# A fixed instruction order from a table, and state transfers with 32 entries outermost

## The chip, the cores and the metric

The kernel runs on one core of one Trainium2 chip. The metric is the device time in microseconds (us): the median of three runs, each one execution of the whole program. A profiled execution gives the trace; its span is the time from the first instruction to the last.

## What is computed

Eight batches go through two stages. In the first, 512 rows of x and 32 rows of state attend to each other, separately for each of 8 heads of width 64. The two results are put one below the other (544 rows). In the second, a mixture of four attention experts runs over those rows, causal, with two experts chosen for each row.

```
x [8, 8, 512, 64], state [8, 8, 32, 64]        # batch, head, row, width
scores  = x @ state^T / 8        ; xread = softmax(scores) @ state       # 512 rows
scores2 = state @ x^T / 8        ; sread = softmax(scores2) @ x          # 32 rows
X = concat([xread, sread], rows), heads side by side                     # [8, 544, 512]
logits = X @ w_gate              ; the two largest of four experts, softmax over the two
for each expert e: q, k, v = X @ wq[e], X @ wk[e], X @ wv[e]
    y = softmax(causal(q @ k^T / 8)) @ v @ wo[e]
    out += (weight of e for the row) * y                                 # [8, 544, 512]
```

## The kernel before, in words

Every value that is multiplied on TensorE (PE) is split into two fp16 parts, high and low, and a product is made of three matmuls (`PROD`). The work of a batch is written as steps. `front(b)` loads x (`xn`) and the state (`sn`), splits x into `xh`, turns it with DMA transposes (`xT`), makes the first softmax (`eb`, `at`), the gate (`lg`, `gt1`, `gt2`, `wgt`; `gate`) and the masked queries, keys and values (`qm`, `kt`, `v`). `side(b)` makes the softmax of the 32 state rows: the exponentials `e2`, the weights `a2`, and their transpose `a2t`. `probs(b, i)` does block i of 128 rows: scores, exponentials `p32`, the split parts `ph`, and a DMA transpose into `pt`. `reads(b, i)` multiplies `pt` with `v`, scales on VectorE (DVE) into `z32`, adds two halves of `z32` on GpSimd (POOL) or DVE, splits the sum into `zh`, transposes it by DMA into `z`, multiplies with `wo_n`, copies the result out of PSUM on ScalarE (ACT) into a tile `o`, and stores it in two stores of 64 rows. `tail(g)` does the state rows of a pair of batches (`tq`, `ptl`, `tpt`, `tzr`, `tz`); every second call stores the 32 state rows of four batches from one tile `o`.

All DMAs are issued by the sync engine (SP), whose queue is in order. `b` in a name of the trace is cut: `p` stands for `p32`, `a` for `a2`, `e` for `e2`, `z` for `z32` and for `z`, `m` for `m2` and `m6`.

Nothing in the code says directly in which order the steps are issued. `Steps.step` records each step with its engine, its estimated duration, and, for some, a choice of engines (`either`). When all are recorded, `Steps.run` orders them: `plan` is a list scheduler with estimated times, `replay` scores a plan with added delays, 12 rounds of forward and backward planning and 100 random changes follow, and the best plan is emitted. The plan decides three things: the order on each engine, the engine where there is a choice, and the buffer slot of each tile. Where it sees PE idle for more than 0.5 us it also puts in filler matmuls on zeros (line 477). Since all steps are emitted in `run`, nearly every row of the trace carries line 479, and the steps are told apart by the names of their tiles.

The two transfers that the change touches are the load of one half of the heads' states and the store of the state rows:

```
st.dma(sns[b // 2][:, b % 2, c], state[b].rearrange("(j c) n d -> c j n d", c=2)[c], 0.6, after=after)
st.dma(out[(g_ - 1) * NB:(g_ + 1) * NB, S:S + NS, :], o, 0.73)
```

In the first, the outermost dimension of the DRAM side is j, four heads; in the second it is the batch, four of them.

Of the kernel before, what the change touches and what calls it, by code (L numbers as in the profile page):

```python
# [15 lines left out]
ALU = mybir.AluOpType  # L16
# [10 lines left out]
LN = math.log(2.0 ** 15)  # L27

# [57 lines left out]
class Steps:  # L86
# [7 lines left out]
    FILL = 0.0535  # L94

    KEEP = 3.0
    START, LANDED, TICK = 0.65, 0.93, 10.24 / 3
    LANDS = (1.4, 2.0, 2.6)
    SIGNAL = {"PE": 0.2, "ACT": 0.16, "DVE": 0.14, "POOL": 0.1, "SP": 0.0}

    def __init__(self, nc, sb, psum):
        self.nc, self.pools, self.tags, self.all = nc, {False: sb, True: psum}, {}, []
        self.base, self.scale, self.clock, self.kind, self.lines = 0.0, 1.0, 0.0, "", {}
        self.behind = None
        self.lean = {"DVE": 0.0, "ACT": 0.0, "POOL": 0.0}
        self.patience = dict.fromkeys(("PE", "DVE", "ACT", "POOL", "SP"), 0.0)
# [17 lines left out]
    def step(self, eng, dur, calls, reads, writes, land=0.0, after=None, ways=None, issue=0.0, modes=(None, None)):  # L124
        s = dict(modes=modes, eng=eng, dur=dur, calls=calls, ways=[(*w, self.takes_port(w[0], w[2])) for w in ways or [(eng, dur, calls, 0.0)]], want=self.base + self.scale * self.clock, n=len(self.all),
# [42 lines left out]
    def dma(self, out, in_, transfer, transpose=False, after=None):  # L168
# [3 lines left out]
        return self.step("SP", max(1.18, transfer + 0.35) if transpose else issue, [(f, dict(out=out, in_=in_))], [v for v in (in_,) if isinstance(v, View)],  # L172
                         [v for v in (out,) if isinstance(v, View)], land=transfer, after=after, issue=issue)
# [32 lines left out]
    def plan(self, want, ways=None, back=False, until=None):  # L206

        steps = self.all  # L210
        after, before = self.links
        then = before if back else after
        waits = [len(x) for x in (after if back else before)]
        ready = [0.0] * len(steps)
        free = dict.fromkeys(("PE", "DVE", "ACT", "POOL", "SP"), 0.0)
        if not back:
            free.update(SP=0.62, POOL=1.14, DVE=1.5, ACT=1.5, PE=0.94)
        dma_free = 0.0
        mode = None
        port = 0.0  # L220
        counts = []
        open_ = {e: [] for e in free}
        pool = {tag: [(0.0, i) for i in range(len(slots))] for tag, slots in self.tags.items()}
        line = {k: (n[0] - 1 if back else 0) for k, n in self.lines.items()}
        fills = {}
        slot, left, last = {}, {i: b.left for i, b in self.bufs.items()}, {}
        used = self.used

        def opens(n):
            for e in ([steps[n]["ways"][ways[n]][0]] if ways else [w[0] for w in steps[n]["ways"]]):  # L230
                open_[e].append(n)

        for n in range(len(steps)):
            if not waits[n]:
                opens(n)

        def start(n):
            t = ready[n]
            need = {}
            for i in used[n]:  # L240
                if i not in slot:
                    b = self.bufs[i]
                    if line[b.turn[0]] != b.turn[1]:
                        return None
                    need[b.tag] = need.get(b.tag, 0) + 1
            for tag, k in need.items():
                p = pool[tag]
                if len(p) < k:
                    return None
                t = max(t, p[k - 1][0])  # L250
            return t

        def held(way):
            return (free["POOL"] if way[0] == "DVE" else port) if way[4] else 0.0

        order = []
        while len(order) < len(steps):
            best = None
            for e, cand in open_.items():
                now, mine = free[e], []  # L260
                for n in cand:
                    t = start(n)
                    if t is None:
                        continue
                    w = steps[n]["ways"]
                    if ways:
                        t = max(t, now, held(w[ways[n]]))
                    else:
                        cost = {x[0]: max(t, free[x[0]], held(x)) for x in w}
                        if len(w) > 1 and e != min(w, key=lambda x: cost[x[0]] + x[1] + x[3])[0]:  # L270
                            continue
                        t = cost[e]
                    mine.append((t, want[n] + (self.KEEP if e == "PE" and steps[n]["modes"][-1 if back else 0] != mode else 0.0), n))
                if mine:
                    t = min(mine)[0] + self.patience[e]
                    t, _, n = min((m for m in mine if m[0] <= t), key=lambda m: m[1:])
                    if best is None or t < best[0]:
                        best = t, n, e
            if best is None and back:

                short = {self.bufs[i].tag for c in open_.values() for n in c for i in used[n] if i not in slot}
                assert short
                for tag in short:
                    pool[tag].append((max(o[3] for o in order), 0))
                continue
            if best is None:
                return 1e9, order, slot, fills
            t, n, e = best
            s = steps[n]
            for i, w in enumerate(s["ways"]):  # L290
                if n in open_[w[0]]:
                    open_[w[0]].remove(n)
                if w[0] == e:
                    way, dur = i, w[1]
            clear = None
            for i in used[n]:
                if i not in slot:
                    b = self.bufs[i]
                    if b.tag == "bank" and clear is None:
                        clear = pool[b.tag][0][0]  # L300
                    slot[i] = pool[b.tag].pop(0)[1]
                    line[b.turn[0]] += -1 if back else 1
            if e == "PE":
                first, last_ = s["modes"][::-1] if back else s["modes"]
                dur += self.SWITCH * (first != mode)
                mode = last_
            end = t + dur
            if e == "PE" and not back and clear is not None:
                at = max(clear, free["PE"])
                if t - at > 0.5:  # L310
                    fills[n] = 0
                    while True:
# [3 lines left out]
                        if at > t - 0.15:  # L316
                            break
# [166 lines left out]
def state_read_then_moe_attention(ctx: ExitStack, tc: tile.TileContext, x, state, w_gate, wq, wk, wv, wo, out):  # L484
# [13 lines left out]
    P = 128  # L498
# [697 lines left out]
```

## Time and profile before

| | |
|---|---|
| three runs | 331.86, 332.98, 334.36 us (median 332.98) |
| profiled execution, span | 329.7 us; the page gives no other time of this execution, so what lies around the span is told by the median, 3.3 us above it |
| PE busy | 301.7 us, 92% |
| DVE busy | 265.6 us, 81% |
| ACT, POOL busy | 212.0 us (64%), 197.5 us (60%) |
| DMA queue 1 | 77.9% of the time of 16 engines |
| mean granted TensorE clock | 0.989 |

PE's busy time overstates its work, since the matmuls are pipelined and one that is held back in the pipeline still counts. A share of a whole span is a mean over stretches with different limits, so it is read by stretches.

### The profile page before, as it was taken

Reading aid. Unit: us, or ns where it says so; the run is one execution under the profiler, and the core shown is the slowest. Engines: PE = TensorE matmul, PEld = TensorE weight load, DVE = VectorE, ACT = ScalarE, POOL = GpSimd, SP = SyncE. Lnnn points to the kernel's source line nnn. Section 1 sums busy time; section 2 is a strip of 40 time slices with the busy share of each in tenths; the row PEclk is TensorE's granted clock in tenths of the full one; section 3 lists DMA queues with packets and bytes.
Section 4 is the critical chain, followed back from the end, with each engine's and each line's share of the span. In section 5 each row is a group of like instructions: output and inputs, shape, how many; then the busy total and the mean of one; then the engine's idle time right before and its main releaser. Section 6 shows DMA issues by size and latency. Waiting matters only on the chain.

```text
span 329.7 us, 10132 instructions
## 1 busy us (share of the span) xinstructions
PE 301.7 (92%) x3906; PEld 201.3 (61%) x3906; DVE 265.6 (81%) x850; ACT 212.0 (64%) x483; POOL 197.5 (60%) x267
## 2 busy tenths in 40 slices
PE   7999599899996999978999997999999999999991
PEld 7786275586454655755456754857546846686750
DVE  3789899999998997995789994998988875894430
ACT  4676697585747859556668874866866756365330
POOL 7044286397864877955868960969965844645400
PEclk9999999999999999999799999999999999999997
DMA  8949909983898999999749898397789867408754
GB/s 192 198 108 164 219 10 166 219 115 66 125 194 196 156 164 154 214 162 233 129 96 148 153 230 116 71 145 156 146 149 188 115 127 119 88 20 171 143 127 95
DMA packets 140712, 47.72 MB, mean 145 GB/s; under 512 B 119672, under 2 KB 136056, under 8 KB 140664
## 3 DMA queue, kind: packets, MB, share of 16 engines
q1 hardware_dynamic: 140664, 47.08, 77.9%
q8 instruction: 30, 0.49, 0.6%
q14 instruction: 18, 0.15, 0.2%
HBM read 11.02 MB, written 8.91 MB: 60 GB/s over the span
## 4 chain that ended last, share of the span: by engine, by line
DVE 37%; PE 27%; ACT 13%; DMA 12%; issue 5%; POOL 4%; SPq 1%; ACTq 0%; DVEq 0%; POOLq 0%
PE bank L479 25%; DVE mx L479 4%; DMA pt<-ph 4%; DVE xh L479 3%; DVE qf L479 3%; DVE gs L479 3%; DVE m L479 3%; DVE a L479 2%; DVE sbm L479 2%; DVE eb L479 2%; DMA p<-in_moe_wo_dram 2%; DVE z L479 2%; ACT xh L479 2%; ACT p L479 2%; DMA xn<-in_x_dram 2%
## 5 line engine op out<-in xcount | busy, mean ns | idle before, releaser
L479 PE MATMUL bank<-kt,qm 64*128 64x128 f16 (+7 forms) x384 | 50.8, 303 | 0.8 <-ACT p L479 0.3
L479 PE MATMUL bank<-v,pt 128*128 128x193 f16 x480 | 44.9, 247 | 2.5 <-DMA pt<-ph 1.3
L479 PE MATMUL bank<-wo_n,z 128*128 128x512 f16 x192 | 45.8, 379 | 0.9 <-DMA z<-zh 0.9
L479 PEld LDWEIGHTS <-pt 128*128 128x128 f16 x480 | 40.2, 98 | 8.0 <-issue 3.2
L479 PE MATMUL bank<-at,gs 128*128 128x512 f16 x192 | 44.6, 379 | 0.0
L479 ACT ACTIVATE p<-bank,mx 128x256 f32<-128x256 f32 (+3 forms) x64 | 31.8, 525 | 15.0 <-DVE mx L479 10.5
L479 POOL TENSOR_TENSOR ph<-p,ph 128x256 f16<-128x256 f32 (+3 forms) x24 | 32.2, 1344 | 9.8 <-ACT ph L479 9.3
L479 PEld LDWEIGHTS <-qm 64*128 64x128 f16 (+1 forms) x384 | 22.3, 96 | 17.4 <-issue 5.1
L479 ACT ACTIVATE o<-bank 128x512 f32<-128x512 f32 x34 | 20.0, 593 | 18.0 <-PE bank L479 17.9
L479 POOL TENSOR_TENSOR qm<-qf,qm 128x512 f16<-128x512 f32 x23 | 26.9, 1187 | 6.2 <-ACT qm L479 4.4
L479 PE MATMUL bank<-gs,at 128*128 128x4 f16 (+1 forms) x384 | 29.9, 218 | 0.7 <-DVE mx L479 0.5
L479 DVE TENSOR_REDUCE mx<-bank 128x1 f32<-128x128 f32 (+3 forms) x64 | 28.2, 475 | 2.5 <-PE bank L479 2.3
L479 PEld LDWEIGHTS <-z 128*128 128x128 f16 x192 | 17.7, 98 | 20.0 <-DMA z<-zh 1.6
L479 PEld LDWEIGHTS <-gs 128*128 128x128 f16 x192 | 17.6, 97 | 19.8 <-issue 1.1
L479 PEld LDWEIGHTS <-at 128*128 128x128 f16 x384 | 23.7, 97 | 5.9 <-issue 1.9
L479 POOL TENSOR_TENSOR zh<-z,zh 128x256 f16<-128x256 f32 x29 | 20.3, 700 | 6.1 <-ACT zh L479 5.6
L479 POOL TENSOR_TENSOR z<-z 128x128 f32<-128x128 f32 x32 | 17.1, 538 | 9.1 <-DVE z L479 4.8
L479 ACT ACTIVATE ph<-p 128x256 f16<-128x256 f32 (+3 forms) x26 | 18.7, 722 | 5.9 <-DMA pt<-ph 5.5
L479 DVE SCALAR_TENSOR_TENSOR xh<-xn,xh 128x512 f16<-128x512 f32 x22 | 18.8, 873 | 4.2 <-ACT xh L479 4.0
L479 ACT ACTIVATE xh<-xn 128x512 f16<-128x512 f32 x32 | 19.1, 626 | 4.5 <-DMA xn<-in_x_dram 4.4
L479 DVE TENSOR_TENSOR qf<-bank,mt 64x512 f32<-64x512 f32 (+1 forms) x32 | 21.1, 684 | 1.1 <-ACT mt L479 0.6
L479 POOL TENSOR_TENSOR eb<-eb,sbm 128x512 f32<-128x512 f32 x14 | 15.0, 1080 | 6.9 <-DVE sbm L479 5.4
(175 smaller groups left out, 677.6 us busy)
## 6 DMA issues: line engine op xcount, KB each, us to landing
xn<-in_x_dram SPq DMA_DIRECT2D x16, 512.0 KB
out_dram<-o SPq DMA_DIRECT2D x64, 128.0 KB
sn<-in_state_dram SPq DMA_DIRECT2D x16, 32.0 KB
p<-in_moe_wo_dram SPq DMA_DIRECT2D x2, 256.0 KB
pt<-ph SPq DMA_TRANSPOSE x32
out_dram<-o SPq DMA_DIRECT2D x2, 256.0 KB
z<-zh SPq DMA_TRANSPOSE x29
xT<-xh SPq DMA_TRANSPOSE x28
```

The lines of the kernel that those rows point to most:

```text
L479: f(**{k: v.ap() if isinstance(v, View) else v for k, v in kw.items()})
```

## The change

The planner (`plan`, `replay`, the search in `run`) is gone. In its place stand two tables. `ORDER` lists all 2036 steps in the order in which they are to be issued, each as number.way.fillers: the number of the step as recorded, which of its engines is taken, and how many filler matmuls go ahead of it. `SLOTS` gives the buffer slot of each tile. Whoever made the tables ran a longer search, with a model of the DMA queue. The code that records the steps is the same but for the two transfers, which have a dimension of 32 state rows outermost, and what follows from that: the partitions of a loaded state are in the order (row, head), and PE's transpose of it is read in another order (`byhead`); the state rows of a pair of batches in `zr` are interleaved (`both`); and one store of four batches is now two stores of two.

```diff
+ORDER = """
+3.0 0.0 1.0 2.0 4.0 68.0 70.0 67.0 11.0 7.0 16.0 12.0 10.0 8.0 17.0 13.0.6 9.0 18.0 14.0 15.1 69.0 21.0 20.0 19.1 22.0 26.0 74.0.23 73.0 27.0 72.0
...
+SLOTS = {
+    "xn": "0101011001101010",
...
-    def run(self, rounds, climbs, tries=8):
...
+    def run(self):
+
+        order = [entry.split(".") for entry in ORDER.split()]
+        left = {i: iter(slots) for i, slots in SLOTS.items()}
+        assert len(order) == len(self.all)
+        for entry in order:
+            s = self.all[int(entry[0])]
+            calls = s["ways"][int(entry[1])][2]
+            for b in s["bufs"].values():
+                if b.slot is None:
+                    b.slot = self.tags[b.tag][int(next(left[b.tag])) if b.tag in left else 0]
+            if len(entry) > 2:
+                to = next(kw["out"].buf.slot for _, kw in calls)
+                for _ in range(int(entry[2])):
                     self.nc.tensor.matmul(out=to[:, :128], lhsT=self.zeros, rhs=self.zeros, start=True, stop=True, skip_group_check=True)
-            for f, kw in s["ways"][way][2]:
+            for f, kw in calls:
                 f(**{k: v.ap() if isinstance(v, View) else v for k, v in kw.items()})
...
-            select(both[r, c * NS:(c + 1) * NS], ALU.not_equal, 1.0, 0, [[-1, NS]], 1)
+            select(both[r, c:NB * NS:NB], ALU.not_equal, 1.0, 0, [[-1, NS]], 1)
...
-            st.dma(sns[b // 2][:, b % 2, c], state[b].rearrange("(j c) n d -> c j n d", c=2)[c], 0.6, after=after)
+            st.dma(sns[b // 2][:, b % 2, c], state[b].rearrange("(j c) n d -> c n j d", c=2)[c], 0.2, after=after, par=(0.2, 8, 0.55))
...
-        hi_lo(P, bd[:, 0], bd[:, 1], tp[:, :P], 128.0)
+        byhead = tp[:, :P].rearrange("p (n j) -> p j n", j=H // 2)
+        hi_lo(P, bd[:, 0].rearrange("p (j n) -> p j n", n=NS), bd[:, 1].rearrange("p (j n) -> p j n", n=NS), byhead, 128.0)
...
-        st.dma(out[(g_ - 1) * NB:(g_ + 1) * NB, S:S + NS, :], o, 0.73)
+        for k in range(2):
+            b0 = (g_ - 1 + k) * NB
+            st.dma(out[b0:b0 + NB, S:S + NS, :].rearrange("b n d -> n b d"), o[k * N:(k + 1) * N], 0.365, par=(0.64, 4, 0.59))
```

The new order stands on every engine. Three places of it are shown, each as it was and as it is. The first is on SP, in the fifth batch, around the first transpose of its state-row weights `a2` (here `a_0`) into `a2t`; `sn` is a state load, `xn` half of a batch's x, `xT` the transpose of a part of x, `out_dram` a store of 64 rows. Before:

```order
L479 DMA_TRANSPOSE z_165<-zh_167 128x4x128
L479 DMA out_dram<-o_170 64x512 x2
L479 DMA sn_87<-in_state_dram 128x1x64
L479 DMA xn_88<-in_x_dram 128x8x128
L479 DMA sn_87<-in_state_dram 128x1x64
L479 DMA_TRANSPOSE xT_97<-xh_96 128x8x128
L479 DMA_TRANSPOSE a2t_145<-a_0_146 128x8x128
L479 DMA xn_89<-in_x_dram 128x8x128
```

After:

```order
L346 DMA_TRANSPOSE xT_97<-xh_95 128x8x128
L346 DMA_TRANSPOSE xT_97<-xh_96 128x8x128
L346 DMA_TRANSPOSE pt_0_156<-ph_150 128x8x128
L346 DMA out_dram<-o_171 64x512
L346 DMA out_dram<-o_170 64x512
L346 DMA_TRANSPOSE a2t_145<-a_0_146 128x8x128
L346 DMA_TRANSPOSE pt_0_157<-ph_149 128x12x128
L346 DMA_TRANSPOSE z_164<-zh_167 128x4x128
```

The loads that stood directly ahead of `a2t` have moved away; the last of them ahead of it is now an `sn` twelve rows earlier, and two stores and a transpose of `ph` stand in front.

The second place is the end of SP's program. Before:

```order
L479 DMA out_dram<-o_171 64x512 x2
L479 DMA out_dram<-o_172 64x512 x2
L479 DMA out_dram<-o_169 64x512 x2
L479 DMA out_dram<-o_170 4x32x512
L1191 UNCONDITIONAL_BRANCH
```

After:

```order
L346 DMA out_dram<-o_170 64x512 x2
L346 DMA out_dram<-o_169 32x2x512 x2
L346 DMA out_dram<-o_172 64x512 x2
L346 DMA out_dram<-o_171 64x512 x2
L1059 UNCONDITIONAL_BRANCH
```

The store of the state rows was the last transfer, with four entries outermost; it is now two stores with 32 entries outermost, and four ordinary stores come behind it.

The third place is on DVE, near its end, where blocks of the last batch are scaled (`z` here is `z32`, `c` its factors, `bank` a PSUM bank). Before:

```order
L479 TENSOR_TENSOR z_0_158<-bank_86,c_0_161 128x384
L479 TENSOR_SCALAR bank_81<-bank_81 128x2
L479 SCALAR_TENSOR_TENSOR z_165<-bank_84,z_165 128x256
L479 RECIPROCAL bank_81<-bank_81 128x2
L479 TENSOR_TENSOR c_1_162<-bank_81,wgt_123 128x6
```

After:

```order
L346 TENSOR_TENSOR z_2_160<-bank_85,c_2_163 128x384
L346 TENSOR_SCALAR bank_80<-bank_80 128x2
L346 TENSOR_TENSOR z_2_160<-z_2_160 128x128
L346 RECIPROCAL bank_80<-bank_80 128x2
L346 TENSOR_TENSOR c_0_161<-bank_80,wgt_123 128x6
```

The sum of the two halves of `z32` (128x128), which POOL did for every block before, is now done by DVE for this block. Over the whole program DVE has 37 instructions more, ACT 22 fewer and POOL 12 fewer; PE has 291 matmuls on zeros in place of 284 (36 of either are the warm-up at the start), and all its other matmuls are the same in number.

More of the change, by code (lines that the diff above doesn't have):

```diff
@@ L92 @@
     SWITCH = 0.1
[L94 to L99, printed above, removed]
     def __init__(self, nc, sb, psum):
@@ L166, in either, with dma @@
         self.step(*ways[0][:2], list(ways[0][2:]), r, w, ways=[(way[0], way[1], list(way[2:]), self.lean[way[0]]) for way in ways])
-    def dma(self, out, in_, transfer, transpose=False, after=None):
+    def dma(self, out, in_, transfer, transpose=False, after=None, par=None):
         f = self.nc.sync.dma_start_transpose if transpose else self.nc.sync.dma_start
         issue = 0.65 if isinstance(in_, View) else 0.475
-        return self.step("SP", max(1.18, transfer + 0.35) if transpose else issue, [(f, dict(out=out, in_=in_))], [v for v in (in_,) if isinstance(v, View)],
-                         [v for v in (out,) if isinstance(v, View)], land=transfer, after=after, issue=issue)
+        n = self.step("SP", max(1.18, transfer + 0.35) if transpose else issue, [(f, dict(out=out, in_=in_))], [v for v in (in_,) if isinstance(v, View)],
+                      [v for v in (out,) if isinstance(v, View)], land=transfer, after=after, issue=issue)
+        if par:
+            self.all[n]["dma"] = par
+        return n
     def mm(self, group, *sizes, into=(), after=None):
@@ L204, in graph @@
         return after, before
[L206 to L312, printed above, removed]
-                        k = int(at / self.TICK)
-                        counts.extend([0.0] * (k + 2 - len(counts)))
-                        at += self.FILL * (1.0 if counts[k] >= 3072 else 2.0)
-                        if at > t - 0.15:
-                            break
-                        counts[k + 1] += 128
-                        fills[n] += 1
-            if e == "PE" and not back:
-                at, work = t, dur
-                while True:
-                    k = int(at / self.TICK)
-                    counts.extend([0.0] * (k + 2 - len(counts)))
-                    slow = 1.0 if counts[k] >= 3072 else 2.0
-                    m = min(work, ((k + 1) * self.TICK - at) / slow)
-                    counts[k + 1] += s["land"] * m / max(dur, 1e-6)
-                    at, work = at + m * slow + 1e-9, work - m
-                    if work <= 1e-9:
-                        break
-                end = at
-            free[e] = end
-            if e == "DVE" and s["ways"][way][4]:
-                port = end
-            if e == "SP":
-                dma_free = max(dma_free, t + s["issue"] + self.START) + s["land"]
-                if s["land"] and dur > s["issue"]:
-                    free[e] = max(end, dma_free - min(0.95, s["land"] + 0.12))
-                end = dma_free + self.LAND
-            end += self.SIGNAL[e]
-            for i in used[n]:
-                last[i] = max(last.get(i, 0.0), end)
-                left[i] -= 1
-                if not left[i]:
-                    bisect.insort(pool[self.bufs[i].tag], (last[i], slot[i]))
-            for o, done in then[n]:
-                waits[o] -= 1
-                ready[o] = max(ready[o], end if done else t)
-                if not waits[o]:
-                    opens(o)
-            order.append((n, way, t, end))
-        return max(o[3] for o in order), order, slot, fills
```

158 lines of the change are left out of this document (40 added, 118 removed), and 88 rows, old and new, of the table ORDER.

## The prediction

> **What bounds the kernel now.** The page's head comes first: the span, the engines' busy shares, and the shares of the chain of waits by engine.
>
> ```profile
> span 329.7 us, 10132 instructions
> PE 301.7 (92%) x3906; PEld 201.3 (61%) x3906; DVE 265.6 (81%) x850; ACT 212.0 (64%) x483; POOL 197.5 (60%) x267
> DVE 37%; PE 27%; ACT 13%; DMA 12%; issue 5%; POOL 4%; SPq 1%; ACTq 0%; DVEq 0%; POOLq 0%
> ```
>
> PE is 92% busy, yet only 27% of the chain that ended last is PE; 37% is DVE. So for long stretches PE does not set the pace. Which ones, the view by windows tells (width, busy us and instructions of PE, weight load, DVE, ACT and POOL, then PE's granted clock, DMA share, GB/s).
>
> ```profile
> 0.00:60.00 60.00, 53.06 (x924) 39.63 (x925) 49.63 (x137) 41.51 (x91) 27.21 (x68) 1.00 0.79 152
> 60.00:210.00 150.00, 137.34 (x1718) 89.04 (x1717) 131.81 (x424) 102.98 (x238) 104.32 (x121) 0.99 0.87 156
> 210.00:322.30 112.30, 111.30 (x1268) 72.60 (x1266) 84.18 (x291) 66.88 (x154) 65.99 (x79) 1.00 0.70 129
> 322.30:329.70 7.40, 0.00 (x1) 0.00 (x0) 0.00 (x0) 0.60 (x1) 0.00 (x0) 0.76 0.35 84
> ```
>
> Four stages with four limits. From 210 on PE is busy 111.3 of 112.3 us: nothing but less PE work shortens that, and the change takes none away. From 60 to 210 PE is idle 12.66 us (150.00 − 137.34) while DVE is busy 131.81, or 88%. The last 7.4 us hold one copy and no other compute. The middle in slices of 15 us:
>
> ```profile
> 60.00:75.00 15.00, 13.60 (x227) 11.08 (x225) 14.83 (x51) 10.04 (x28) 11.24 (x12) 1.00 0.87 155
> 75.00:90.00 15.00, 13.54 (x169) 7.99 (x167) 14.97 (x50) 10.47 (x24) 12.15 (x14) 1.00 0.62 96
> 90.00:105.00 15.00, 12.85 (x149) 7.61 (x147) 12.97 (x42) 7.85 (x17) 7.17 (x9) 1.00 1.08 208
> 105.00:120.00 15.00, 13.63 (x173) 9.40 (x174) 14.67 (x36) 10.75 (x25) 12.98 (x14) 1.00 0.91 147
> 135.00:150.00 15.00, 12.69 (x167) 9.95 (x163) 14.90 (x67) 8.42 (x19) 10.06 (x15) 1.00 0.99 183
> 150.00:165.00 15.00, 13.34 (x139) 7.02 (x139) 8.91 (x28) 9.54 (x23) 10.85 (x14) 0.89 0.92 169
> 195.00:210.00 15.00, 12.94 (x141) 7.93 (x139) 10.34 (x31) 9.70 (x21) 4.33 (x7) 1.00 0.73 129
> ```
>
> Two sorts of slice lose PE time. In those at 60, 75, 105 and 135 DVE is busy 14.7 to 15.0 of 15: PE waits for DVE, 6.5 us in all (1.40 + 1.46 + 1.37 + 2.31). In those at 90, 150 and 195 DVE is itself idle while PE is: 2.15 + 1.66 + 2.06 = 5.9 us, and there something else is late. The chain of waits (start, us, what) names it in two of them and near the third:
>
> ```profile
> 137.64 5.34 DMA pt<-ph
> 149.57 4.81 DMA a2t<-a
> ...
> 197.95 3.92 DMA pt<-ph
> ...
> 244.43 58.00 PE bank L479 x680
> ```
>
> They are DMA transposes that take 4 to 5 us from issue to landing. The last row shows that from 244 to 302 the chain is PE alone.
>
> **The change, part by part.** All terms are set against the span, 329.7; the median of the three runs shown, 332.98, lies 3.3 above it, and I add the 3.3 at the end.
>
> *The end.* The timeline (start, us, engine, instruction; in brackets the idle time ahead and its releaser) has the last copies, and the windows behind them:
>
> ```profile
> 321.04 0.60 ACT L479 ACTIVATE o<-bank 128x512 f32<-128x512 f32 x1 [0.70 <-PE bank L479]
> 322.39 0.60 ACT L479 ACTIVATE o<-bank 128x512 f32<-128x512 f32 x1 [0.75 <-PE bank L479]
> ```
>
> ```profile
> 323.50:324.00 0.50, 0.00 (x0) 0.00 (x0) 0.00 (x0) 0.00 (x0) 0.00 (x0) 1.00 0.95 213
> 324.00:324.50 0.50, 0.00 (x0) 0.00 (x0) 0.00 (x0) 0.00 (x0) 0.00 (x0) 1.00 0.18 45
> 327.00:327.50 0.50, 0.00 (x0) 0.00 (x0) 0.00 (x0) 0.00 (x0) 0.00 (x0) 0.50 0.26 102
> 328.00:328.50 0.50, 0.00 (x0) 0.00 (x0) 0.00 (x0) 0.00 (x0) 0.00 (x0) 0.50 0.15 57
> 328.50:329.00 0.50, 0.00 (x0) 0.00 (x0) 0.00 (x0) 0.00 (x0) 0.00 (x0) 0.50 0.00 0
> ```
>
> The last copy ends at 322.99, 6.7 us ahead of the end. The ordinary stores in flight run at a share of 0.95 and are gone at about 324.1, some 2.5 us after the copy that ended at 321.64. The state rows' store then runs alone at a share of about 0.26, a quarter of the 16 engines, until about 328.3; from there 1.4 us lead to the end. In the new order the last stores are ordinary ones of 64 rows: 2.5 + 1.4 = 3.9 us, call it 4.0. Term: 4.0 − 6.7 = **−2.7**. Bounds: −1.7 if the 32-entry stores ahead are still in the way for a microsecond, −3.3 if the last two stores land sooner, with less in flight than four had.
>
> A rule of the Trainium skill bears on that share ("DMA: Bandwidth & Descriptors", section "Why a DMA increments its semaphore by 16 and not by 1"): a transfer is spread over the largest number of engines, up to 16, that divides the slowest dimension of both sides. By it four entries get four engines, and 32 get 16; the share of 0.26 agrees for four, and no run shown here has the 32.
>
> *The first a2t of the fifth batch.* In SP's queue, and then on the engines:
>
> ```profile
> 146.67 0.51 SPq L479 DMA_DIRECT2D xn<-in_x_dram  x1
> ...
> 147.94 1.53 SPq L479 DMA_TRANSPOSE xT<-xh  x1
> 149.57 1.27 SPq L479 DMA_TRANSPOSE a2t<-a  x1
> ...
> 154.46 0.72 ACT L479 ACTIVATE a<-e,s 128x512 f16<-128x512 f32 x1 [2.90 <-DMA a2t<-a]
> ...
> 155.21 0.75 DVE L479 SCALAR_TENSOR_TENSOR a<-e,s,a 128x512 f16<-128x512 f32 x1 [3.14 <-ACT a L479]
> ```
>
> ```profile
> 158.90:162.20 3.30, 3.30 (x20) 1.26 (x19) 2.90 (x11) 2.17 (x5) 2.47 (x4) 0.50 0.64 135
> ```
>
> `a2` has one buffer. ACT writes the second `a2` only after the first transpose has read it, and that stood behind a 512 KB load of x, two state loads and `xT`. ACT waits 2.90, DVE behind it 3.14, PE loses the 1.66 us of its slice, and then it runs 3.3 us at half clock, worth 1.65. After the change no load stands directly ahead of that transpose; two stores of 128 KB and a transpose of `ph` do. Term: −(1.66 + 1.65) = **−3.3**; bounds 0 (the stores hold it as long as the loads did) and −4.8, the whole transfer in the chain.
>
> *The rest of 60 to 210.* Of PE's 12.66 us idle, 11.0 are left. The 5.9 − 1.66 = 4.2 with DVE idle are the sort that an order with the DMA queue in mind can mend: loads moved ahead, transposes issued sooner. The 6.5 behind a full DVE go only if DVE work is moved to where DVE has room, and the new order has some 2 us more on DVE in this part, not less. I take half: **−5.5**, which is about the first sort and a fifth of the second. Bounds 0 and −11.0.
>
> *Added work.* DVE has 37 instructions more. They are priced by these groups (busy us and mean ns of one behind the bar):
>
> ```profile
> L479 POOL TENSOR_TENSOR z<-z 128x128 f32<-128x128 f32 x32 | 17.1, 538 | 9.1 <-DVE z L479 4.8 <-DVE bank L479 2.3 <-DVE gs L479 0.9
> L479 DVE TENSOR_TENSOR tqf<-bank,tmt 128x128 f32<-128x128 f32 x8 | 1.9, 276 | 0.1
> L479 DVE SCALAR_TENSOR_TENSOR v<-bank,v 128x256 f16<-128x256 f32 x32 | 12.9, 414 | 1.9 <-ACT v L479 1.6
> L479 DVE TENSOR_TENSOR qm<-qf,qm 128x512 f16<-128x512 f32 x1 | 0.7, 686 | 0.0
> L477 PE MATMUL bank<-zeros 128*128 128x128 bf16 x248 | 15.9, 221 | 3.3 <-ACT e L479 3.2
> ```
>
> Seven sums of `z32` halves come over from POOL; no DVE row has them, and their size is that of `tqf`: 7 × 0.276 = 1.9, or 7 × 0.538 = 3.8 if they cost what POOL takes, the other end. Five remainders of `zh`, as wide as `v`: 5 × 0.414 = 2.1. Three each of `qm` and `at`, 128x512: 6 × 0.686 = 4.1. The other 19 at the mean DVE instruction, 265.6/850 = 0.31: 5.9. Sum 14 us, about 2 of it ahead of the place that ran at 210 us and 12 behind. Behind, DVE is busy 84.18 of 112.30, so 28 us of idle DVE cover it: term **0**, bounds 0 and +8.5 (rival D). ACT loses 22 instructions (about 10 us at its mean of 0.44) and POOL 12 (9 us at 0.74); neither bounds, so 0. Seven more fillers, 7 × 0.22 = 1.5 us, stand in the first fifth of PE's program, where PE was idle 60 − 53.06 = 6.9 us anyway: 0, bounds −6.9 (that idle gone) and +1.5. State loads, spread wider, land sooner by less than the 5.50 us that the first x takes, which is ahead of everything; 0.
>
> ```profile
> 1.25 5.50 DMA xn<-in_x_dram
> ```
>
> A rule that speaks against the change stands in the Trainium skill ("GPSIMD Engine Reference", "Specifications"): GpSimd shares its SBUF interfaces with VectorE, with contention where a DVE instruction has two SBUF inputs. The moved sums and remainders have two. In this trace the 128x512 `xh` with two SBUF inputs takes 873 ns and the `kt` from PSUM 683:
>
> ```profile
> L479 DVE SCALAR_TENSOR_TENSOR xh<-xn,xh 128x512 f16<-128x512 f32 x22 | 18.8, 873 | 4.2 <-ACT xh L479 4.0
> L479 DVE SCALAR_TENSOR_TENSOR kt<-bank,kt 128x512 f16<-128x512 f32 x16 | 10.9, 683 | 2.9 <-ACT kt L479 2.9
> ```
>
> The rows agree, but do not tell contention from the operands' own cost. With 0.19 us on some 15 more such instructions the sum would be 2.9 longer, if nothing covered them.
>
> Sum: 329.7 − 2.7 − 3.3 − 5.5 = 318.2 of span; with 3.3 around it **321.5**.
>
> **The rivals.**
>
> A. Only the end gains. PE idle in the middle comes from DVE at 88%; an order moves the waits, and what goes at one place returns at the next. For it: most of that idle stands behind a full DVE, and DVE has more to do after. Against: three DMA waits with DVE idle. 329.7 − 2.7 + 3.3 = **330.3**.
>
> B. The middle becomes as dense as the stretch behind 210. −2.7 − 12.66 − 1.65 leaves 312.7, and 3.3 make **316.0**. For it: the last third shows that PE can be busy 99%. Against: DVE there is 75% busy, not 88%.
>
> C. The change of shape doesn't do what it says: the state rows' stores stay at a quarter of the engines, hold the last ordinary ones up, and the end stays at 6.7. 321.5 + 2.7 = **324.2**. Against it: the dimension is 32 on both sides.
>
> D. Slower, by DVE in the last third. With 12 us more DVE is busy 96 of 112.3 there, 86%; at 88% in the middle PE was idle 8.4% of the time. If the last third goes the same way, 8.4% of 112.3 are 9.5 us where 1.0 is now: +8.5, with nothing won in the middle: 329.7 − 2.7 + 8.5 + 3.3 = **338.8**. It decides once DVE has a queue of work ahead of what PE waits for, and not before; even in the middle, PE was busy all of some slices. Against it: the moved steps are off PE's shortest path, sums and remainders that have until their transposes.
>
> **How the numbers follow.** The forecast gets 0.50, A 0.17, B 0.14, C 0.07, D 0.12. One per cent, 3.3 us, is about what a measurement of this kernel can tell from no change, so the limits are 329.6 and 336.3. Faster: the forecast, B, C (0.71) and 0.02 of A's spread. Same: 0.14 of A and 0.03 of D. Slower: 0.09 of D and 0.01 of A. The range leaves out the tail of B with the start's idle gone as well, and most of D: 313 to 335, that is all of the forecast's own bounds of the middle term (316.0 to 327.0).
>
> **What would show it.** From the end of the last copy into `o` to the end of the span 4.0 us. In the fifth batch no wait of ACT for `a2t`, and no stretch at half clock. The DMA share never at a quarter while nothing else runs. In the 150 us ahead of the last third PE idle about 5 in place of 12.7, and the rows behind PE's idle time DVE rather than DMA. DVE busy near 280. I am wrong if PE's idle time reappears in the last third with DVE beyond 86% (D), if the middle keeps its 12 us behind other releasers (A), or if the start grows by more than the fillers, since I took it as level.

## The result, and the profile after

The changed kernel takes **321.02 us** (median of 4 runs, 320.16 to 322.67) against 332.97 for the kernel before (4 runs beside it): a ratio of 0.966, 95% interval 0.961 to 0.972. The prediction said 321.5. The span of the profiled execution is 318.4 us, 11.3 less than before. Where a kernel below had executions in a slower state of the chip (two of twelve in run 7, one of six in run 6), its median is that of the others.

The head of the page of the changed kernel, in the order of the rows shown of before:

```profile
span 318.4 us, 10154 instructions
PE 297.3 (93%) x3913; PEld 200.2 (63%) x3913; DVE 270.0 (85%) x887; ACT 202.1 (63%) x461; POOL 186.8 (59%) x255
PE 37%; DVE 28%; DMA 19%; ACT 5%; issue 4%; POOL 3%; SPq 3%; ACTq 0%; POOLq 0%; DVEq 0%
```

PE has 37% of the chain of waits in place of 27, DVE 28 in place of 37, DMA 19 in place of 12. By windows, with the last two stages cut where the changed kernel's own end begins:

```profile
0.00:60.00 60.00, 54.64 (x948) 40.52 (x949) 49.55 (x135) 41.20 (x90) 28.00 (x68) 1.00 0.73 147
60.00:210.00 150.00, 141.41 (x1853) 93.96 (x1851) 137.43 (x463) 102.02 (x238) 107.02 (x125) 1.00 0.94 172
210.00:314.44 104.44, 101.23 (x1117) 65.75 (x1114) 83.06 (x290) 58.92 (x135) 51.76 (x63) 1.00 0.65 121
```

In the same 150 us PE gets through 1853 matmuls in place of 1718 and is idle 8.6 us in place of 12.7; the DMA share is 0.94 in place of 0.87. The stretch behind it holds 1117 matmuls in place of 1268, and is less dense: 3.2 us idle in 104.4. (The matmuls on zeros of the changed kernel all stand before 60 us.)

What PE waited for from 60 to 210 us changed in kind. The longest rows of before, and then of the changed kernel (waiter, releaser: us in all, times, longest):

```profile
PE bank L479 <- DMA a2t<-a: 2.1, 1, 2.1
PE bank L479 <- DVE tmx L479: 1.4, 1, 1.4
PE bank L479 <- DMA pt<-ph: 1.3, 1, 1.3
```

```profile
PE bank L346 <- DMA pt<-ph: 2.1, 2, 1.3
PE bank L346 <- DMA a2t<-a: 1.7, 2, 1.3
PE bank L346 <- DVE m L346: 1.5, 2, 1.2
PE bank L346 <- DMA xT<-xh: 1.5, 1, 1.5
```

Over all waits of these 150 us, those for DVE fell from 6.3 to 2.0 us and those for ACT from 2.8 to 0.7, while those for DMA rose from 3.3 to 5.3.

The end: the last copy into `o`, and the windows behind it.

```profile
313.84 0.60 ACT L346 ACTIVATE o<-bank 128x512 f32<-128x512 f32 x1 [0.70 <-PE bank L346]
```

```profile
314.50:315.00 0.50, 0.00 (x0) 0.00 (x0) 0.00 (x0) 0.00 (x0) 0.00 (x0) 1.00 0.84 193
316.50:317.00 0.50, 0.00 (x0) 0.00 (x0) 0.00 (x0) 0.00 (x0) 0.00 (x0) 1.00 0.64 143
317.00:317.50 0.50, 0.00 (x0) 0.00 (x0) 0.00 (x0) 0.00 (x0) 0.00 (x0) 1.00 0.00 0
```

The copy ends at 314.44, 3.96 us ahead of the end (4.0 was forecast, 6.7 it was). The share falls from 0.64 to nothing with no stretch at a quarter.

### The profile page after: what moved, and what is told of

Read it like the earlier page. It is cut to its first block, busy times and chain, and to the rows that moved or that the text cites. A ratio compares the mean times of both kernels' runs of the same rounds, so it can differ in the third digit from the quotient of the medians.

```text
span 318.4 us, 10154 instructions
## 1 busy us (share of the span) xinstructions
PE 297.3 (93%) x3913; PEld 200.2 (63%) x3913; DVE 270.0 (85%) x887; ACT 202.1 (63%) x461; POOL 186.8 (59%) x255
## 4 chain that ended last, share of the span: by engine, by line
PE 37%; DVE 28%; DMA 19%; ACT 5%; issue 4%; POOL 3%; SPq 3%; ACTq 0%; POOLq 0%; DVEq 0%
PE bank L346 37%; DMA pt<-ph 6%; DMA z<-zh 5%; DMA a2t<-a 3%; DVE qf L346 3%; DVE sbm L346 3%; DVE mx L346 3%; SPq L346 3%; DMA p<-in_moe_wk_dram 2%; DVE eb L346 2%; DVE m L346 2%; DVE xh L346 2%; DVE mb L346 2%; DMA sn<-in_state_dram 2%; ACT ph L346 2%
## 5 line engine op out<-in xcount | busy, mean ns | idle before, releaser
L346 PE MATMUL bank<-kt,qm 64*128 64x128 f16 (+7 forms) x384 | 49.5, 300 | 0.1
L346 ACT ACTIVATE p<-bank,mx 128x128 f32<-128x128 f32 (+3 forms) x64 | 31.2, 524 | 20.0 <-DVE mx L346 14.7
L346 POOL TENSOR_TENSOR ph<-p,ph 128x256 f16<-128x256 f32 (+3 forms) x19 | 26.9, 1417 | 18.4 <-ACT ph L346 12.5
L346 PE MATMUL bank<-gs,at 128*128 128x256 f16 (+1 forms) x384 | 30.4, 218 | 0.3 <-POOL at L346 0.3
L346 POOL TENSOR_TENSOR z<-z 128x128 f32<-128x128 f32 x25 | 12.8, 512 | 24.7 <-DVE z L346 14.4
L346 POOL TENSOR_TENSOR qm<-qf,qm 128x512 f16<-128x512 f32 x20 | 23.3, 1180 | 5.4 <-ACT qm L346 5.2
L346 POOL TENSOR_TENSOR zh<-z,zh 128x256 f16<-128x256 f32 x24 | 17.8, 743 | 11.8 <-ACT zh L346 7.2
L346 ACT ACTIVATE ph<-p 128x512 f16<-128x512 f32 (+3 forms) x22 | 16.4, 748 | 5.7 <-DMA pt<-ph 5.5
L346 DVE TENSOR_TENSOR z<-bank,c 128x384 f32<-128x384 f32 x32 | 17.6, 551 | 0.6
L346 DVE SCALAR_TENSOR_TENSOR xh<-xn,xh 128x512 f16<-128x512 f32 x19 | 14.6, 782 | 3.9 <-ACT xh L346 3.9
```

Of the source, the lines that this page charges most:

```text
L346: f(**{k: v.ap() if isinstance(v, View) else v for k, v in kw.items()})
```

## The experiments

They are told by what they belong to; the labels of the expectations give the order in which they ran (where they name others, e1 is run 1 and e3 is run 5 here). Every kernel is written as a table of order, engine and slot, so that one thing can be changed and all else held. Each ran beside the kernel before, and a ratio is against that (its median was 331.9 to 332.6 in these runs). ORDER entries are number.way.fillers.

**1. The shapes alone.** The plan of the kernel before, written out, with the two new transfers:

```diff
 ORDER = """
-3.0 0.0 1.0 2.0 4.0 68.0 70.0 67.0 11.0 7.0 16.0 12.0 10.0 8.0 17.0 13.0.6
+3.0 0.0 4.0 1.0 2.0 67.0 68.0 69.0 70.0 71.0 72.0 73.0 11.0 5.0 6.0 16.0
...
```

> The order, engines and buffer slots of the kernel before, written out as a table, with only the state loads and the state-row stores of the change (32 entries outermost). Theory: of the 12 us the shape gives the end alone, 6.7 us from the last copy into o to the end of the span become about 4.0, so 332.98 - 2.7 = 330.3 us. Rival 1, the shape does nothing and the end was won by putting ordinary stores last: 333.0, and a share of about 0.26 still stands at the end. Rival 2, the state loads count too, since in the kernel before 4 of 16 engines carried them ahead of other transfers: below 329.

Measured: 330.07 us, ratio 0.993 (0.990 to 0.996), 2.5 us less. The state-row stores still come last here, and the end is as short as in the changed kernel:

```profile
span 327.3 us, 10135 instructions
```

```profile
322.69 0.60 ACT L344 ACTIVATE o<-bank 128x512 f32<-128x512 f32 x1 [0.75 <-PE bank L344]
```

The copy ends at 323.29, 4.0 us ahead of 327.3. The shape does it, wherever the store stands. Rival 1 is out, and so is rival 2 (below 329): in this order no more is won than the end.

**2. The new order with the old shapes.**

```diff
-            st.dma(sns[b // 2][:, b % 2, c], state[b].rearrange("(j c) n d -> c n j d", c=2)[c], 0.2, after=after, par=(0.2, 8, 0.55))
+            st.dma(sns[b // 2][:, b % 2, c], state[b].rearrange("(j c) n d -> c j n d", c=2)[c], 0.6, after=after)
...
-        for k in range(2):
-            b0 = (g_ - 1 + k) * NB
-            st.dma(out[b0:b0 + NB, S:S + NS, :].rearrange("b n d -> n b d"), o[k * N:(k + 1) * N], 0.365, par=(0.64, 4, 0.59))
+        st.dma(out[(g_ - 1) * NB:(g_ + 1) * NB, S:S + NS, :], o, 0.73)
```

> The order, engines and slots of the changed kernel with the two transfers as before: loads with four heads outermost, and one store of the state rows of four batches, four entries outermost, in the place of the first of the two. Theory: the quarter-speed store starts ahead of four ordinary stores and ends beside them, so the end gains most of its 2.7 us even so; time 321.0 to 322.5. Rival, the shape carries the whole end term wherever the store stands: 321.0 + 2.7 = 323.7. If the state loads matter, more than 324.

Measured: 326.24 us, ratio 0.982 (0.978 to 0.986). That is 5.2 us above the changed kernel, more than either the theory or the rival gave for the end. In the new order the shapes are worth about twice what they are in the old. The expectation put anything above 324 down to the state loads; the next two runs ask whether that is so.

**3. The old state load alone, and 4. the old state-row store alone,** each in the changed kernel (for 3 the lines ahead of the dots in the diff above, for 4 those behind them, and the layouts that go with each).

> The changed kernel with the state loads alone as before, four heads outermost. Both shapes undone gave 326.2 against 321.0. Theory after that run: the state loads carry the part that is not the end: the first state arrives 1.3 us later and others hold transfers up, so 323 to 325. By the sum on record, which gave the state loads nothing: 321.0.

> The changed kernel with the state-row store alone as before: one store of four batches, four entries outermost, where the first of the two stands. Theory: the end goes from 4.0 to 5.4 us from the last copy, as with both shapes undone, 322.4. Rival, the quarter-speed store of the first four batches, in the middle, holds up transposes as well: 323.5 or more. Rival, position alone matters: 321.0.

Measured: 322.87 us (ratio 0.972, 0.968 to 0.976) with the old load, 325.80 (0.981, 0.977 to 0.985) with the old store. The load's interval overlaps that of the changed kernel, and its span is 319.1 beside 318.4: whether 1.9 us are its worth stays open, and neither the 321.0 nor the 323 of its expectation is ruled out. The store is worth 4.8, the rival's way (323.5 or more), and the end is only part of that: its last copy starts at 317.48 and the span is 323.6, so 5.5 us lie behind the copy in place of 3.96. With the same order on PE, the copies into `o` are milestones that can be set beside each other in two traces. Two in a row of the changed kernel, and the same two with the old store:

```profile
228.19 0.59 ACT L346 ACTIVATE o<-bank 128x512 f32<-128x512 f32 x1
239.82 0.60 ACT L346 ACTIVATE o<-bank 128x512 f32<-128x512 f32 x1 [2.93 <-PE bank L346]
```

```profile
229.71 0.59 ACT L344 ACTIVATE o<-bank 128x512 f32<-128x512 f32 x1
...
244.09 0.60 ACT L344 ACTIVATE o<-bank 128x512 f32<-128x512 f32 x1 [2.01 <-PE bank L344]
```

The first is 1.5 us late though neither store has run yet; executions of one program can lie further apart than that (runs 9 and 12 have the same instructions up to about 150 us, and their first copies stand at 86.33 and 88.75). The second is 4.3 late. Between them, 2.8 us are lost in this pair of traces, and there stands the other state-row store, that of the first four batches. From the first to the second copy the changed kernel takes 11.6 us, runs 3, 9, 10 and 11 take 11.4 to 12.0 and run 12 takes 13.0; with the old store it is 14.4 here and 13.6 in run 2. SP's queue with the old store, and the chain of waits:

```profile
227.97 1.27 SPq L344 DMA_DIRECT2D out_dram<-o  x2
229.34 3.14 SPq L344 DMA_TRANSPOSE pt<-ph  x1
```

```profile
229.34 7.19 DMA pt<-ph
```

```profile
236.57 2.12 PE L344 MATMUL bank<-v,pt 128*128 128x193 f16 x12 [2.63 <-DMA pt<-ph]
```

```profile
230.00:231.00 1.00, 1.00 (x12) 0.89 (x10) 0.80 (x4) 1.00 (x4) 0.92 (x3) 1.00 0.15 12
236.40:239.40 3.00, 2.83 (x28) 1.94 (x36) 1.05 (x6) 2.24 (x4) 1.66 (x1) 0.50 1.10 230
```

One of the two stores at 227.97 is that of the state rows. The `pt` behind it takes 7.19 us from issue to landing, and in the second from 230 the DMA share is 0.15, with 12 GB/s moved. PE waits 2.63 us and then runs 3 us at half clock. In the changed kernel the same `pt` takes half as long (and 3.2 to 3.4 us in runs 9, 10 and 12, which have the new store; 6.83 in run 2, which has the old one):

```profile
228.39 3.55 DMA pt<-ph
```

The place differs a little as well. In the changed kernel one half of this store goes out ahead of the a2t in front of it, and the old store stands whole in the place of the other half, so 128 KB more are directly ahead of the `pt`. At the 230 GB/s of the last window that is 0.6 us (an estimate), of the 3.6 by which the `pt` is longer. A narrow store is not the only thing that makes a transpose late, either: in run 12 the next `pt` took 6.35 us with the new store.

So the store on few engines has a price at two places: at the end, where nothing but the end waits for it, and in front of a transpose that PE needs, about 2 to 3 us. The prediction priced the first only. In the old order the second cost nothing that run 1 could show; the new order put a needed transpose there.

**5. The a2t of the fifth batch.** In the kernel before, SP alone:

```diff
 DMA out_dram<-o_170 64x512 x2
+DMA_TRANSPOSE xT_97<-xh_96 128x8x128
+DMA_TRANSPOSE a2t_145<-a_0_146 128x8x128
 DMA sn_87<-in_state_dram 128x1x64
 DMA xn_88<-in_x_dram 128x8x128
 DMA sn_87<-in_state_dram 128x1x64
-DMA_TRANSPOSE xT_97<-xh_96 128x8x128
-DMA_TRANSPOSE a2t_145<-a_0_146 128x8x128
```

> The kernel before in all but one place: in the fifth batch the two state loads and the 512 KB load of x stand behind the first a2t on SP, not ahead of it and of the xT before it. Theory: the wait of ACT of 2.9 us and the stretch at half clock go, 333.0 - 3.3 = 329.7 us, with a2t landing about 3 us after its issue in place of 4.8. Rival: the time won comes back at the next wait, since DVE is the bound around it: 332.5 to 333.5 even where the wait is gone. A second rival: the loads come too late for batch 6, and it gets slower than 333.

Measured: 330.01 us, ratio 0.993 (0.991 to 0.996), 2.5 us less. The place itself, in ACT's timeline (no wait stands in brackets) and by the window that had PE 13.34 us busy at a mean clock of 0.89:

```profile
152.08 0.73 ACT L344 ACTIVATE a<-e,s 128x512 f16<-128x512 f32 x1
```

```profile
150.00:165.00 15.00, 15.00 (x201) 8.40 (x199) 12.19 (x38) 11.91 (x28) 12.53 (x14) 1.00 0.84 176
```

ACT's wait is gone, PE is busy throughout and the clock is whole. What became of it, copies into `o` tell, first of this kernel, then of before:

```profile
165.63 0.60 ACT L344 ACTIVATE o<-bank 128x512 f32<-128x512 f32 x1
177.36 0.58 ACT L344 ACTIVATE o<-bank 128x512 f32<-128x512 f32 x1
...
320.67 0.60 ACT L344 ACTIVATE o<-bank 128x512 f32<-128x512 f32 x1 [0.75 <-PE bank L344]
```

```profile
168.72 0.59 ACT L479 ACTIVATE o<-bank 128x512 f32<-128x512 f32 x1
178.29 0.57 ACT L479 ACTIVATE o<-bank 128x512 f32<-128x512 f32 x1
```

3.09 us are won at the first, 0.93 are left at the second, and at the last 1.72 (320.67 against 322.39). Ahead of the place this execution was 0.64 us late (150.25 against 149.61), so the place may have given 3.7; single traces are no firmer than that. Behind the place DVE is full (14.84 of the 15 us from 165), and the wait is now PE's for DVE, which before had none here:

```profile
179.09 0.86 PE L344 MATMUL bank<-identh,m 128*64 128x128 f16 x24 [1.52 <-DVE m L344]
```

**6. Both of these together,** the shapes and the a2t, in the old order.

> The order of the kernel before with the new shapes (e1) and with the a2t of the fifth batch ahead of the three loads (e3). Each alone was worth 2.5 us. Theory: they stand at different places, so they add: 332.6 - 5.0 = 327.6 us. Rival: the loads of the state, now spread, no longer held a2t up, so e1 has part of e3 in it: 328.5 to 330.

Measured: 327.69 us, ratio 0.985 (0.981 to 0.989), 4.7 less. They add within what can be told. So these two account for 4.7 of the 12 us in this order; the rest comes only with the new order, engines and slots.

**7. The new order with the engines of before, and 8. the old order with the engines of after.** The edit is the second number of 119 entries of ORDER: in the first every step has its way of before, in the second its way of after.

> The changed kernel with each step on the engine it had before (DVE 37 instructions fewer, ACT 22 and POOL 12 more), in the new order of steps and slots. Theory, the order gives the gain and the engines are neutral: 321 to 323. Rival, the choice of engines is part of the gain, since POOL and ACT were late with sums, remainders and casts: 325 or more. Rival D turned round, the 37 instructions on DVE cost time: below 320.

> The order and slots of the kernel before, with the new shapes, and each step on the engine that the changed kernel gives it (where e1 keeps the old engines). With the new order the old engines gave back all of the gain. Theory: order and engines are one solution and neither is worth anything alone, so this is slower than the 330.1 of the same order with its own engines: 332 to 342 us. Rival 1, the engines are the gain: 322 or less. Rival 2, they are neutral in this order: 329 to 331.

Measured: 332.85 us (ratio 1.001, 0.998 to 1.005) and 348.36 (1.048, 1.043 to 1.053). The first expectation's theory (321 to 323) fell and its rival (325 or more) stands; the second went the way of its theory, and beyond its 342. With the new shapes in all four, and the slots of their order, the square is

| | engines of before | engines of after |
|---|---|---|
| order of before | 330.07 | 348.36 |
| order of after | 332.85 | 321.02 |

Neither is worth anything without the other: each alone costs 3 and 18 us, together they win 9. In the worst corner PE waits for DVE more and longer than in the same order with its own engines. Of run 1, and then of run 8:

```profile
PE bank L344 <- DVE gs L344: 1.4, 4, 0.4
PE bank L344 <- DVE m L344: 1.1, 3, 0.6
```

```profile
PE bank L344 <- DVE m L344: 8.2, 4, 3.8
PE bank L344 <- DVE gs L344: 3.8, 3, 2.5
```

This is slower by waits for DVE, as rival D had it, but not where D had it: the first copy into `o` is already 8.7 us late (101.13 against 92.43 before) of the 18.8 at the last, and behind 210 us DVE is busy 103.85 of 131.8, which is 79% and not D's 86. That the steps added to DVE are what delays these pieces is likely, and not shown. Engines carried over into an order are a crude test: each was planned for its own order, so the square shows that they belong together, not which single step does it.

**9. Twelve steps back on POOL.**

```diff
-482.1 495.1 969.1 971.1 1223.1 1272.1 1437.1 1488.1 1708.1 1710.1 1757.1 1947.1
+482.0 495.0 969.0 971.0 1223.0 1272.0 1437.0 1488.0 1708.0 1710.0 1757.0 1947.0
```

They stand in ORDER one by one; way 1 is DVE, way 0 POOL. Seven add halves of `z32`, five split off the remainder of `zh`.

> The changed kernel with twelve steps back on POOL that it put on DVE: the seven sums of z32 halves and the five remainders of zh. Theory by the sum on record, DVE work behind 210 us is covered: 321.0 either way, within 1 us. Rival D, two SBUF inputs on DVE cost more than they bring: below 319.8. Other rival, POOL was late with them (ACT waited 9.0 us for POOL's sums before): 322.5 or more.

Measured: 320.56 us, ratio 0.964 (0.961 to 0.968): no difference. These twelve were the clearest part of DVE's added work. They are covered, as the sum said, and they are no part of the gain either.

**10 to 12. Can the trace of the changed kernel be read for more?** Three places where its PE waits for a transpose, moved by the pattern of run 5:

```diff
-DMA_TRANSPOSE a2t_145<-a_0_146 128x8x128
 DMA_TRANSPOSE xT_97<-xh_95 128x8x128
...
+DMA_TRANSPOSE a2t_145<-a_0_146 128x8x128
...
-DMA out_dram<-o_171 64x512
-DMA out_dram<-o_170 64x512
...
+DMA out_dram<-o_171 64x512
+DMA out_dram<-o_170 64x512
...
-DMA xn_88<-in_x_dram 128x8x128
...
+DMA xn_88<-in_x_dram 128x8x128
```

> The changed kernel with three moves on SP at places where its trace shows PE waiting for a transpose: at 57.4 us an a2t goes behind the two xT that stood behind it; at 154.0 two stores go behind the a2t and the pt that stood behind them; at 199.0 a 512 KB load of x goes behind the pt that stood behind it. Theory from the a2t run, where 3.1 us won at the place left 1.8 at the end: PE's waits there are 1.5, 1.25 and 0.9, so at most 3.6 at the places and about 2 at the end: 319 us. Rival: the waits return a few steps later, since the a2t and the load are then late: 320.5 to 322.

> The three moves on SP together with the twelve sums and remainders of z back on POOL (which alone gave 320.6, no difference). Theory: the twelve steps stay neutral, so the same as the three moves alone within 1 us. Rival: DVE is the bound again once the waits for transposes are shorter, and 1 us or more is won.

Measured: 325.13 us (ratio 0.976, 0.973 to 0.980) and 324.91 (the same ratio): 4 us slower than the changed kernel, worse than both the theory (319) and the rival (up to 322), and the same with the twelve steps on either engine, as expected. By the copies into `o`, the two are 2.5 and 1.5 us late by 88 us, behind the place of the a2t; around the two stores 0.3 are won in both, but run 3 gains as much there with no move; and between 184 and 211, around the load, 2.7 are lost in both. The a2t that went behind two `xT` is what PE waits for next, 2.06 us where it had waited 1.48 for `xT`:

```profile
64.23 1.57 PE L344 MATMUL bank<-a2t,xh 128*128 128x64 f16 x48 [2.06 <-DMA a2t<-a]
```

For the load I thought of a second `pt` behind it, and moved it behind both, with the a2t back in its place:

> The three moves gave 325.1 in place of 321.0. By the times of its copies into o, the first (a2t behind xT) cost 2.5 us, the second (stores behind pt) won 0.3, the third cost 2.7: there a load of x stood behind one pt but ahead of the next, and PE waited 2.5 for that one. Here the first move is taken back, the second stays, and the load goes behind both pt; the z steps are on POOL as in the kernel that took 320.6. Theory: what stands ahead of the next transpose is the price; with none ahead PE's wait of 0.9 at 206 us goes, 319.5 to 320.6. Rival: the load is needed soon after, so the wait moves to ACT's xh and the time is 322 or more.

Measured: 327.11 us, ratio 0.985 (0.981 to 0.989). The theory fell and the rival stands, on ACT:

```profile
210.79 0.63 ACT L344 ACTIVATE xh<-xn 128x512 f16<-128x512 f32 x1 [4.69 <-DMA xn<-in_x_dram]
211.33 1.55 ACT L344 ACTIVATE mt<-bank 128x512 bf16<-128x512 f32 x3
```

```profile
207.40:212.00 4.60, 0.09 (x2) 0.11 (x2) 0.08 (x2) 1.21 (x3) 0.49 (x1) 1.00 0.85 169
212.00:215.20 3.20, 3.20 (x20) 2.71 (x19) 3.14 (x5) 2.48 (x6) 3.12 (x4) 0.50 0.20 40
```

ACT waits 4.69 us for x, and `mt`, which PE needs for a bank, is behind it in ACT's queue. PE, DVE and POOL all but stand for 4.6 us, and 3.2 us at half clock follow; the copies into `o` are 4.9 us later behind it than ahead of it. The load was in front of the `pt` because it was due; in run 5 the loads moved were not. In the three moves, too, ACT waited for this load (2.68 us, ahead of the same `xh`), so the second `pt` was not what had cost the 2.7. This kernel is also 1.15 us late by 88 us without the move of the a2t, and run 9, with the same instructions as run 12 up to there, is 1.27 early, so what that move cost by itself stays open; it won nothing that can be told. No version here beats the changed kernel by more than can be told from no change.

## Why the prediction was right, point by point

The time came out as forecast, 321.02 for 321.5, and the span too, 318.4 for 318.2. The 3.3 us put around the span were not around it: every execution in these runs took 1.7 to 2.2 us more than its own span, and the rest is that the profiled execution of before was among its faster ones. Of the signs named ahead, the end, the a2t (ACT has no wait for it there, the clock is whole) and the DMA share came true. PE idle about 5 us in the middle did not (8.6), nor DVE busy near 280 (270), nor PE's waits being for DVE rather than DMA, which came out the other way round.

**The end** was right as a mechanism and a size: 6.7 to 3.96 us, 2.75 won for 2.7. Run 1 shows the shape as its cause, with 2.5 us in time. The price of the shape was not the whole of its worth: in the new order it is 5.2 (run 2), because the store of the first four batches stands ahead of a transpose (run 4). The step that failed here is that the store was sized at its last instance alone. The 0 for the state loads is not refuted (run 3). By the rule of the Trainium skill ("DMA: Bandwidth & Descriptors", section "Why a DMA increments its semaphore by 16 and not by 1"), 4 entries outermost keep a transfer to 4 engines and 32 allow 16. The traces agree: a share of 0.26 alone at the end before, and no such stretch at the end of the changed kernel.

**The a2t** was sized at 3.3, the loss at its place. The place gave 3.1, the end of the span kept 1.7 and the time 2.5. What the term left out is what comes late next: PE waited 1.5 us for DVE behind it.

**The rest of the middle**, 5.5, had the least ground; its reason failed, and its size came out by luck. The reason was that the new order mends waits for transposes (4.2 of the 5.5) and leaves most of PE's waits for DVE. The waits of PE show the reverse: for DVE and ACT 9.0 us became 2.7 (1.66 of the 9.0 stood behind the a2t, where ACT and DVE had waited themselves), and for DMA 3.3 became 5.3. These rows name only what PE waited for directly, but the chain of waits, which follows each wait back, goes the same way: DVE from 37 to 28%, ACT from 13 to 5, DMA from 12 to 19. So what the order and the choice of engines mended is in the main what stood behind DVE and ACT. The size is a sum of amounts that offset each other. By the windows PE's idle time from 60 to 210 fell by 4.1, of which 1.66 is the a2t's; that leaves 2.4 where I took 5.5. The start gave 1.6 (idle 6.94 to 5.36) where I took 0, and behind 210 1.5 came back (idle up to the last copy 1.7 to 3.2). PE's busy time fell by 4.4 with 7 matmuls more, 1.65 of it the half clock; the other 2.8 us may be waits inside what the trace calls busy, which no view shows. Together 2.4 + 1.6 − 1.5 + 2.8 = 5.3, each part of it no firmer than the 1 to 2.4 us by which two executions differ at one place.

**The half clock** had a term for one place only, 1.65 us. The 61 executions of before beside these runs have mean clocks of 0.975 to 0.990, with a median of 0.985, and the four of the changed kernel 0.992 to 1.000. At 0.985, 2 × 0.015 × 330 = 10 us ran at half clock; in the profiled execution some 3.6 of those lie behind PE's last work. So a typical execution had about 6 us of PE's time at half clock, and lost about 3 us by it (an estimate). Part of the gain is then that the new order's waits seldom bring the half clock, where the prediction had one place of one trace.

Split by cause in place of by stage, the sum was off by 2.5 both ways: shapes 5.2 where I had 2.7, order and engines 6.3 (332.5 − 326.2) where I had 8.8.

**Added work at no cost** held (run 9). DVE is busy 270.0, not near 280, since other steps took less (`a`, eleven times in both, 8.8 us in place of 10.9; `xh`, 19 in place of 22, 14.6 in place of 18.8). The added steps were dearer than the rows I took:

```profile
L346 DVE TENSOR_TENSOR zh<-z,zh 128x256 f16<-128x256 f32 x5 | 3.9, 781 | 0.0
L346 DVE TENSOR_TENSOR qm<-qf,qm 128x512 f16<-128x512 f32 x4 | 3.4, 848 | 0.0
L346 DVE TENSOR_TENSOR z<-z 128x128 f32<-128x128 f32 x7 | 2.4, 348 | 0.0
```

348 ns for a sum lies between my ends of 276 and 538; 781 for a remainder of `zh` is far from the 414 of `v`, which reads PSUM. The least durations, 274 and 409, are about the prices I gave; the surplus is waiting for POOL, which the last section shows. So the contention that the prediction named was there, and its 2.9 us for some 15 instructions was a fair size: these sums, remainders, `qm` and `at`, 19 in all, waited some 3 us (an estimate from their means and least durations). Run 9 shows for twelve of them that this cost no time. The price of a filler was misread: 221 ns is the duration of one of the matmuls on zeros, which overlap, and 15.9 us for 248 is 0.064 each, so seven are 0.45 us and not 1.5. The term was 0 either way.

**The rivals.** A (the middle's idle stays) and C (the shape does nothing) are out by the result and by run 1. B is out too: PE is still idle 8.6 us of the 150. D did not happen in the changed kernel, where DVE behind 210 is busy 83.1 of 104.4 us and PE idle 3%; run 8 is slower by DVE, but at other places. That the order is one with its engines I had not among the rivals.

## What to carry to other kernels

Price a transfer on few engines at each place where it stands, by what is queued behind it, and not at the end alone. Take the waits by who releases them, and not from whether an engine is full in the same slice: the slices of before put half of PE's idle time down to something other than DVE, while of PE's own waits three quarters were for DVE and ACT, and that is the part that went. Before a transfer is moved, read when its own consumer is due: a load that blocks a transpose is free to move only if the engine that waits for it is not in order ahead of what PE needs. And in a planned kernel, order and choice of engine are one answer; a trace shows where a wait is, but not that the piece ahead of it could go.

## What the runs showed of the hardware that I had not expected

DVE instructions with two SBUF inputs have no fixed duration. Of the changed kernel two rows, and then of before one (minimum, median and maximum in ns):

```profile
L346 DVE SCALAR_TENSOR_TENSOR xh<-xn,xh x19: 677/684/1647, 5.6 to 218.2; 128x512 f16<-128x512 f32 x19
L346 DVE SCALAR_TENSOR_TENSOR kt<-bank,kt x16: 659/682/693, 27.9 to 264.1; 128x512 f16<-128x512 f32 x16
```

```profile
L479 DVE SCALAR_TENSOR_TENSOR xh<-xn,xh x22: 664/713/1657, 5.6 to 209.5; 128x512 f16<-128x512 f32 x22
```

`xh` and `kt` do the same arithmetic at the same size, with nearly equal least durations; `kt` reads one input from PSUM and stays within 34 ns, `xh` reads both from SBUF and reaches 1647. So part of DVE's busy time is waiting, and the trace of the changed kernel shows for whom. A remainder of `zh` with POOL busy ahead of it, that POOL instruction, and a remainder with POOL idle:

```profile
256.12 1.34 DVE L346 TENSOR_TENSOR zh<-z,zh 128x256 f16<-128x256 f32 x1
256.02 1.16 POOL L346 TENSOR_TENSOR at<-et,at 128x512 f16<-128x512 f32 x1 [3.27 <-ACT at L346]
201.60 0.41 DVE L346 TENSOR_TENSOR zh<-z,zh 128x256 f16<-128x256 f32 x1
```

POOL's instruction began first and ended at 257.18; DVE's ended 0.28 us behind that. The same holds for all 11 prolonged ones among the `xh`, `zh`, `z`, `qm` and `at` with two SBUF inputs on DVE: a POOL instruction was running when each began, and each ended 0.14 to 0.15 us (128x128), 0.27 to 0.28 (128x256) or 0.54 to 0.56 (128x512) behind the end of it. None of the others from 9 us on began more than 0.11 us ahead of the end of a running POOL instruction. `kt` began 0.4 and 0.3 us ahead of such an end, at 91.60 and 169.11, and took 0.68 and 0.69. The Trainium skill ("GPSIMD Engine Reference", "Specifications") has GpSimd and VectorE share SBUF interfaces, with contention where a DVE instruction has two SBUF inputs. The trace agrees, and in it DVE waits for the whole of the POOL instruction; no run took POOL's work away to test it.

The half clock came back behind waits of PE, but the length of a wait did not decide it. In before it followed three waits of 1.66 us in all, in run 4 waits of 2.03 and of 2.63 us, and in run 12 one of 4.51; a wait of 2.54 in run 12 and one of 2.06 in run 10 left the clock whole. The old order has a wait of 3.2 us near 41 us. In run 1 the clock was at half behind it, and in run 6, whose program is the same up to there, it was not. The same 48 matmuls in run 1 and in run 6:

```profile
42.56 2.76 PE L344 MATMUL bank<-a2t,xh 128*128 128x64 f16 x48
```

```profile
41.84 1.56 PE L344 MATMUL bank<-a2t,xh 128*128 128x64 f16 x48
```

Most stretches at half clock lasted 3 to 4 us, that of run 1 about 7 (mean clock 0.57 from 40 to 48). It made PE 2.1 us later: run 1 was 0.35 us behind run 6 when it began and 2.48 at its end. So a wait of PE cost its own length and up to about 2 us more, and one execution had such a stretch where another, with the same wait, had none.
